# Rotated q and k of the next head pair: the steps of their preparation tied to units of the pair in front

## The chip, the core and the metric

The kernel runs on one core of one Trainium2 chip. A core has five engines with queues of their own that are worked off in order: TensorE (PE in the profile, its weight loads PEld), VectorE (DVE), ScalarE (ACT), GpSimd (POOL) and SyncE (SP), which here issues all DMAs. The metric is the device time of one execution in microseconds; lower is better.

## The reference, cut to what matters

Attention over 4 batches x 8 heads x 576 tokens x 64 channels with a rotary embedding on q and k, then two layers of a two-matrix network on the 2304 tokens:

```
q_rot, k_rot = rotate(q), rotate(k)            # x1*cos - x2*sin, x1*sin + x2*cos
scores = scale * q_rot @ k_rot^T ; scores -= max(scores)
attn = exp(scores) / (sum(exp(scores)) + 1e-9) ; x = attn @ v
h = x @ w_in  (512 -> 2048) ; g = piecewise square of h ; x = g @ w_out
h = x @ w_in2 ; r = max(h, 0) ; out = (s * r*r + b) @ w_out2
```

## The kernel before

**Attention, by pairs and units.** The 32 heads are worked in 16 pairs (one batch, two heads on 64 + 64 partitions). A pair has 9 units of 128 rows of the score matrix (`UNITS`; the fifth unit holds the last 64 rows of both heads). For each unit `qk` lets PE form the scores in one of two PSUM buffers (`sc`), DVE takes the negated maximum (`nm`, L359), ACT the exponential (`p`, L364); two units later PE transposes the result (`tp`), DVE or ACT copies it out (`pt`), and PE multiplies by v (`av`). Scores of a unit can start when the exponential two units earlier has freed its PSUM buffer. Units and pairs are counted from 0 here; "the fourth unit" is k == 3.

**q and k of a pair.** Each is loaded as a tile of 128 x 2 x 576 f32 (the value and its half-swapped copy) into a ring of 4 buffers, `qkin`. `rope_pair` multiplies by the table (POOL, 4 pieces of 288 columns by `pool_tt`, L96), adds the two halves (for q on DVE, L294; for k on POOL, 2 pieces), and splits the result into a rounded part and a low remainder, because PE multiplies in fp32r. For q, `lay_q` does this per head: an ACT copy scaled by 0.125 (L308), then a DVE subtraction (L309), straight into `qs_t[i % 2]`. For k, `lay_k` does one ACT cast (L321), 2 POOL subtractions (the low part), and then 4 DMAs that lay the rounded part into `kh` (L326) and 2 DMAs that lay the low part into `kz` (L329).

**Order of the work.** The main loop runs over units n = 9*i + k and calls in the order "qltaf": scores, loads and preparation (`do_load`), transposes, products with v, and fill. From n = 48 on fill puts matmuls of the first network between the units; between n = 33 and 106 `convert` splits weights (ACT, DVE and POOL). Which instruction stands where in an engine's queue is fixed before the run by a planner with its own clock: it takes the earliest written instruction whose inputs are ready by that clock. `tc.issue_after(x)` only says that an instruction may not stand ahead of x on x's engine. In the kernel before, the preparation of pair i + 1 is written at k == 0 (q) and k == 2 (k) of pair i, from pair 2 on without any tie. The planner therefore hoists it: in the trace the table product of q of pair i + 3 runs during pair i, the sum right behind it, and the parts of q and the DMAs of k for pair i + 2 stand at the turn from pair i to pair i + 1, when the last scores of pair i have freed `qs_t`, `kh` and `kz`. Pair 0 has its own, already tied order.

After attention (some 440 us) three stages of the networks follow, in which PE runs over weights and tokens.

Of the kernel before, what the change touches and what calls it, by code (L numbers as in the profile page):

```python
# [14 lines left out]
ALU = mybir.AluOpType  # L15
# [51 lines left out]
def kernel(ctx, tc, qq, kk, vv, tab, ww1, ww2, s, b, out):  # L67
    nc = tc.nc
# [16 lines left out]
    def pool_tt(out, in0, in1, op, dim=-1):  # L85

        n = out.shape[dim]
        free = 1
        for x in out.shape[1:]:
            free *= x  # L90
        k = min(n, -(-free // PW))
        for i in range(k):
            c = [slice(None)] * len(out.shape)
            c[dim] = slice(n * i // k, n * (i + 1) // k)
            c = tuple(c)
            m = nc.gpsimd.tensor_tensor(out=out[c], in0=in0[c], in1=in1[c], op=op)  # L96
        return m
# [15 lines left out]
    exps, tps, maxs = {}, {}, {}  # L113

    class Slice:
# [6 lines left out]
        def convert(self, raw, pools, hi, lo):  # L122
            if not wide:
                split(hi, lo, raw, nc.scalar, nc.gpsimd)
                return


            top = raw.bitcast(F32).rearrange("p (n t) -> p n t", t=2)[:, :, 1]
            low = raw.bitcast(U16).rearrange("p (n t) -> p n t", t=4)[:, :, 1]
            pool = pools[self.f * 2 + self.made & 1 if len(pools) > 1 else 0]  # L130
            a = pool.tile([P, HW], F32, tag="wa", name="wa", bufs=WB)
            m = pool.tile([P, HW], F32, tag="wm", name="wm", bufs=WB)
            au, mu = a.bitcast(U32), m.bitcast(U32)
            nc.scalar.activation(a, top, AF.Copy, scale=2.0 ** -112)
            nc.vector.tensor_scalar(out=mu, in0=au, scalar1=3, scalar2=None, op0=ALU.logical_shift_left)
            nc.vector.scalar_tensor_tensor(out=mu, in0=au, scalar=0x80000000, in1=mu, op0=ALU.bitwise_and, op1=ALU.bitwise_or)
            nc.vector.tensor_scalar(out=au, in0=mu, scalar1=0xFF800000, scalar2=None, op0=ALU.bitwise_and)
            nc.vector.scalar_tensor_tensor(out=a, in0=low, scalar=2.0 ** -36, in1=a, op0=ALU.mult, op1=ALU.mult)
            nc.scalar.copy(hi, m)  # L139
            pool_tt(out=m, in0=m, in1=hi, op=ALU.subtract)  # L140
            pool_tt(out=lo, in0=m, in1=a, op=ALU.add)
# [106 lines left out]
    tab_sb = att.tile([P, 2, S], F32, name="tab_sb")  # L248
# [4 lines left out]
    qk_in, v_in, stacks = {}, {}, {}  # L253

    WHOLE = [slice(0, S)]
    HALVES = [slice(0, 288), slice(288, S)]

    def load_qk(i, nm, pieces=WHOLE):
        bb, hp = divmod(i, NP)
        t = att2.tile([P, 2, S], F32, tag="qkin", name=f"{nm}in", bufs=QB)  # L260
        for c in pieces:
            nc.sync.dma_start(out=t[:, :, c], in_=(qq if nm == "q" else kk)[bb, hp, :, :, c])
        qk_in[nm, i] = t

    def load_v(i):
        bb, hp = divmod(i, NP)
        t = att2.tile([P, 5, 2, D], F32, tag="vin", name="vin", bufs=VB)
        for out, src in ((t[:, :, 1], vv[bb, hp, :, :, 1]), (t[:D, :4, 0], vv[bb, hp, D:, :4, 0]), (t[D:, :4, 0], vv[bb, hp, :D, 1:, 0]), (t[D:, 4, 0], vv[bb, hp, :D, 0, 0])):
            nc.sync.dma_start(out=out, in_=src)
        v_in[i] = t  # L270
# [15 lines left out]
    def rope_pair(i, nm, mul, add, lo_eng, pieces=WHOLE):  # L286

        t = qk_in[nm, i]
        tt = {nc.gpsimd: pool_tt, nc.vector: nc.vector.tensor_tensor}
        last = None  # L290
        for c in pieces:
            tt[mul](out=t[:, :, c], in0=t[:, :, c], in1=tab_sb[:, :, c], op=ALU.mult)
            r = t[:, 1, c]
            tt[add](out=r, in0=t[:, 0, c], in1=r, op=ALU.add)  # L294
            last = (lay_q if nm == "q" else lay_k)(i, t, c, lo_eng)
        return last

    SELF = [slice(0, D), slice(D, P)]
    laid, parts = set(), {}

    def lay_q(i, t, c, lo_eng, heads=range(2)):

        st = stacks["q", i] = qs_t[i % 2]
        r = t[:, 1, c]
        for j in heads:
            own, other = SELF[j], SELF[1 - j]
            at = slice(j * QW + c.start, j * QW + c.stop)
            h = nc.scalar.activation(st[own, at], r[own], AF.Copy, scale=0.125)  # L308
            m = nc.vector.scalar_tensor_tensor(out=st[other, at], in0=r[own], scalar=0.125, in1=st[own, at], op0=ALU.mult, op1=ALU.subtract)  # L309
        return h.ins, m.ins  # L310

    def lay_k(i, t, c, lo_engs, heads=range(2)):
        if (i, "k") not in laid:
            laid.add((i, "k"))
            stacks["k", i] = att.tile([P, 2, S], F32R, tag="kh", name="kh", bufs=2), kz_t[i % 2]
        kh, kz = stacks["k", i]
        tt = {nc.gpsimd: pool_tt, nc.vector: nc.vector.tensor_tensor}
        r = t[:, 1, c]
        if i > 0:
            hi, lo = t[:, 0, c].bitcast(F32R), r.bitcast(F32R)  # L320
            cast = nc.scalar.copy(hi, r)  # L321
            low = pool_tt(out=lo, in0=r, in1=t[:, 0, c], op=ALU.subtract)
            parts[i] = cast.ins, low.ins
            for j in range(2):
                for rows in SELF:
                    m = nc.sync.dma_start(out=kh[rows, j, c].bitcast(F32), in_=t[SELF[j], 0, c])  # L326
            with tc.issue_after(m.ins):
                for j in range(2):
                    m = nc.sync.dma_start(out=kz[SELF[j], j, c].bitcast(F32), in_=t[SELF[j], 1, c])  # L329
            return m.ins  # L330
        for j in heads:
            own, other = SELF[j], SELF[1 - j]
            nc.scalar.copy(kh[own, j, c], r[own])
            m = nc.scalar.copy(kh[other, j, c], r[own])
            low = tt[lo_engs[j]](out=kz[own, j, c], in0=r[own], in1=kh[own, j, c], op=ALU.subtract)
        return m.ins, low.ins
# [192 lines left out]
    def turned_by(t, c):  # L529
        nc.vector.tensor_tensor(out=t[:, :, c], in0=t[:, :, c], in1=tab_sb[:, :, c], op=ALU.mult)  # L530
        return nc.vector.tensor_tensor(out=t[:, 1, c], in0=t[:, 0, c], in1=t[:, 1, c], op=ALU.add).ins
# [53 lines left out]
    def do_load(n):  # L585
        if n == 0:
            with tc.issue_after(turned):
                turned_by(tq, QP[1])
                lay_q(0, tq, QP[1], None)
        elif n in (1, 2):  # L590
            with tc.issue_after(maxs[n]):
                if n == 1:
                    turned_by(tq, QP[2])
                else:
                    lay_q(0, tq, QP[2], None)
        if n < len(units):
            i, k = units[n]
            if i + 1 < NPAIR:
                if i == 0 and k in (2, 6):
                    with tc.issue_after(maxs[k]):  # L600
                        turned_by(qk_in["q", 1], HALVES[k // 6])
                if i == 0 and k in (4, 5, 7, 8):
                    with tc.issue_after(maxs[k]), tc.issue_after(exps[k - 1]):
                        lay_q(1, qk_in["q", 1], HALVES[k // 6], None, [int(k in (5, 8))])
                if i and k == 0:
                    with ExitStack() if i > 1 else tc.issue_after(parts[1][1]), ExitStack() if i > 1 else tc.issue_after(maxs[9]):
                        rope_pair(i + 1, "q", nc.gpsimd, nc.vector, None)
                elif k == 2:
                    with ExitStack() if i else tc.issue_after(exps[2]), ExitStack() if i else tc.issue_after(lowest):
                        rope_pair(i + 1, "k", nc.gpsimd, nc.gpsimd, [nc.gpsimd, nc.vector])  # L610
                elif k == 7:
                    load_v(i + 1)
                elif k in (4, 6) and i + 2 < NPAIR:
                    load_qk(i + 2, "q" if k == 4 else "k")

        if n in range(33, 51, 2) or n in range(70, 110, 4):
            with tc.issue_after(exps[n - 14]):
                convert()

        if n in PARK_AT and parking:  # L620
            with tc.issue_after(exps[n - 4]):
                parking.pop(0).park(wst, scratch)()
# [31 lines left out]
    def do_fill(n):  # L654
        if n < 48:
            return
        with tc.issue_after(exps[min(n, len(units)) - 4]):
            run_fill(0.62 if n < 76 else 0.92)

    acts = {"q": do_qk, "l": do_load, "t": do_t, "a": do_av, "f": do_fill}  # L660
    for n in range(len(units) + LA):
        with ExitStack() as st:
# [541 lines left out]
```

## Time and profile before

| | |
|---|---|
| median of 3 runs | 1116.61 us (1113.03 to 1118.2) |
| the profiled execution | 1117.65 us, span 1115.9 us, granted TensorE clock 0.998 |
| busy share of the span | PE 96%, PEld 88%, DVE 69%, ACT 57%, POOL 38% |
| pairs 1 to 14, whose code changes | from 33 us to about 440 us |

A row of the trace reads: start in us, length in us, engine, line, operation, out<-in, shapes, count, and in brackets the idle time of the engine before it with what ended it. Rows of waits read: engine, line, what it waited for, then total us, number of times and longest.

### The profile page before, as it was taken

The numbers are of one execution on the slowest core, as the hardware profiler recorded it, in microseconds if no ns is written. First come the engines' busy times: TensorE is split into PE (matmuls) and PEld (weight loads), VectorE is DVE, ScalarE is ACT, GpSimd is POOL, SyncE is SP. The second block draws the span as 40 slices with busy tenths as digits, with TensorE's granted clock in tenths as the row PEclk, the third lists the DMA queues.
The fourth block names the chain that finished last, engine by engine and source line by source line (L and its number), as shares of the span: only waits on it lengthen the run. The fifth ranks groups of instructions, "written<-read, shape, count | busy, mean of one in ns | idle before, by whom it ended". The sixth has DMA issues, their size and how long they took to land.

```text
span 1115.9 us, 20052 instructions
## 1 busy us (share of the span) xinstructions
PE 1074.3 (96%) x7296; PEld 981.3 (88%) x7296; DVE 775.0 (69%) x1445; ACT 631.0 (57%) x1440; POOL 426.9 (38%) x564
## 2 busy tenths in 40 slices
PE   5899999989999999999999999999999999999998
PEld 3666788878888889999999999999999999999997
DVE  7888987768576663454757667866777778677754
ACT  5777776766666665454545455474554448334431
POOL 6998977686473332332544445110212110000000
PEclk9999999999999999999999999999999999999999
DMA  8665856656675544655465673231322853221221
GB/s 240 168 191 167 253 160 208 207 165 188 202 227 166 174 151 138 220 171 190 149 183 203 211 238 116 86 112 59 113 89 90 301 171 116 82 83 42 80 63 36
DMA packets 109762, 173.24 MB, mean 155 GB/s; under 512 B 29408, under 2 KB 80608, under 8 KB 109664
## 3 DMA queue, kind: packets, MB, share of 16 engines
q1 hardware_dynamic: 109664, 171.97, 49.1%
q8 instruction: 57, 0.93, 0.4%
q14 instruction: 41, 0.34, 0.1%
HBM read 110.10 MB, written 48.56 MB: 142 GB/s over the span
## 4 chain that ended last, share of the span: by engine, by line
PE 81%; DVE 5%; DMA 5%; POOL 3%; ACT 3%; issue 2%; SPq 0%; POOLq 0%; ACTq 0%
PE hps L181 15%; PE sum L940 14%; PE yps L856 6%; PE yps L855 6%; PE yps L854 6%; PE y L181 5%; PE sc L357 5%; PE yps L790 4%; PE yps L791 4%; PE yps L792 4%; PE av L405 4%; PE h L181 4%; PE tp L379 3%; DMA wraw<-in_ww 1%; DMA kz<-kin 1%
## 5 line engine op out<-in xcount | busy, mean ns | idle before, releaser
L181 PE MATMUL hps<-xh,w 128*128 128x288 f32 (+4 forms) x640 | 163.4, 324 | 0.0
L357 PE MATMUL sc<-kh,qs 128*128 128x288 f32 x336 | 102.7, 328 | 24.5 <-ACT p L364 13.5
L359 DVE TENSOR_REDUCE nm<-sc 128x1 f32<-128x576 f32 x144 | 106.5, 748 | 24.9 <-PE sc L357 24.4
L364 ACT ACTIVATE p<-sc,nm 128x576 f32<-128x576 f32 x144 | 106.7, 742 | 28.6 <-DVE nm L359 26.2
L948 ACT ACTIVATE four<-four,b_sb,s_sb 128x480 f32<-128x480 f32 x64 | 47.4, 782 | 127.2 <-DVE four L947 127.2
L856 PE MATMUL yps<-gh,w 128*128 128x480 f32 (+1 forms) x320 | 118.5, 370 | 0.0
L854 PE MATMUL yps<-gh,w 128*128 128x480 f32 (+1 forms) x320 | 118.4, 370 | 0.0
L855 PE MATMUL yps<-gl,w 128*128 128x480 f32 (+1 forms) x320 | 118.4, 370 | 0.0
L96 POOL TENSOR_TENSOR wm<-wm,w 128x256 f32<-128x256 f32 x80 | 69.5, 888 | 119.1 <-ACT w L139 62.5
L181 PEld LDWEIGHTS hps<-xh,w 128*128 128x128 f32 x640 | 113.2, 188 | 1.0
L357 PEld LDWEIGHTS sc<-kh,qs 128*128 128x128 f32 x336 | 63.5, 192 | 45.7 <-ACT p L364 27.0
L181 PE MATMUL hps<-xl,w 128*128 128x288 f32 (+4 forms) x320 | 103.7, 324 | 0.0
L790 PE MATMUL yps<-gh,w 128*128 128x288 f32 (+3 forms) x288 | 93.2, 324 | 1.4 <-DVE yp L797 0.7
L357 PE MATMUL sc<-kz,qs 128*128 128x288 f32 x336 | 93.8, 301 | 0.0
L791 PE MATMUL yps<-gl,w 128*128 128x288 f32 (+3 forms) x288 | 92.8, 322 | 0.0
L792 PE MATMUL yps<-gh,w 128*128 128x288 f32 (+3 forms) x288 | 92.8, 322 | 0.0
L379 PE MATMUL tp<-ident,p 128*128 128x128 f32 x576 | 87.2, 276 | 4.0 <-DVE pt L386 3.4
L96 POOL TENSOR_TENSOR wm<-wm,raw 128x256 f32<-128x256 f32 x16 | 12.6, 806 | 176.8 <-ACT raw L139 176.8
L181 PE MATMUL y<-gh,w 128*128 128x288 f32 x320 | 75.0, 305 | 2.0 <-DVE ptr L397 0.9
L379 PEld LDWEIGHTS tp<-ident,p 128*128 128x128 f32 x576 | 70.5, 142 | 6.2 <-DVE pt L386 4.1
L405 PE MATMUL av<-pt,vin 128*64 128x256 f32 (+1 forms) x512 | 75.7, 417 | 0.0
L107 DVE TENSOR_TENSOR gl<-hps,gh 128x288 fp32r<-128x288 f32 (+4 forms) x88 | 46.4, 527 | 40.4 <-ACT gh L103 40.2
(154 smaller groups left out, 2905.9 us busy)
## 6 DMA issues: line engine op xcount, KB each, us to landing
wraw<-in_ww SPq DMA_DIRECT2D x56, 512.0 KB, 4.4
w<-parkd SPq DMA_DIRECT2D x24, 512.0 KB, 6.1
kin<-in_k SPq DMA_DIRECT2D x15, 576.0 KB, 4.4
qin<-in_q SPq DMA_DIRECT2D x15, 576.0 KB, 4.8
kh<-kin SPq DMA_DIRECT2D x60, 144.0 KB, 2.9
parkd<-wraw SPq DMA_DIRECT2D x16, 512.0 KB, 3.2
xs<-y1d SPq DMA_DIRECT2D x32, 240.0 KB, 2.7
xd<-u SPq DMA_DIRECT2D x16, 288.0 KB, 2.7
```

The lines of the kernel that those rows point to most:

```text
L181: m = nc.tensor.matmul(out_ps, l, r, start=(i == 0), stop=(i == n - 1))
L357: nc.tensor.matmul(sc[:, half, o:o + n], l, r[:, k0:k0 + n], start=m == 0, stop=m == len(todo) - 1)
L364: exps[i * 9 + k] = nc.scalar.activation(p, sc[:, :, :288], AF.Exp, bias=nm, scale=1.0, accum_out=sums_t[i][:, col:col + 1]).ins
L379: m = nc.tensor.transpose(v[:, c, :], p[:, c * P:(c + 1) * P], ident)
L405: nc.tensor.matmul(ps[j * D:(j + 1) * D, :n], v[:, kt, j, :], pt[g][:, kt, j, :], start=kt == 0, stop=False)
L790: nc.tensor.matmul(acc, wh, gh, start=f == 0, stop=False)
L791: nc.tensor.matmul(acc, wh, gl, start=False, stop=False)
L792: nc.tensor.matmul(acc, wl, gh, start=False, stop=last)
L854: nc.tensor.matmul(acc, wh, gh, start=f == 0, stop=False)
L855: nc.tensor.matmul(acc, wh, gl, start=False, stop=False)
L856: nc.tensor.matmul(acc, wl, gh, start=False, stop=last)
L940: nc.tensor.matmul(acc, l, r, start=j == 0, stop=j == len(t) - 1)
```

## The change

For pairs i >= 1 the call of `rope_pair` is taken apart. q of pair i + 1: the table product on POOL stays written at k == 0; the DVE sum is written at k == 4 behind the maximum of the unit before (k == 3); the two heads' parts are written at k == 5 and k == 6, their DVE half behind the maximum of the unit before and their ACT half behind the exponential two units before. k of pair i + 1: product and sum on POOL stay at k == 2; cast, low part and the six DMAs are written at k == 3, the cast behind the exponential of k == 2. The tie that q's sum of pair 2 had to the maximum of unit 9 is gone with the call.

```
+                if i:
+                    t = qk_in["q", i + 1]
+                    if k == 0:
+                        with ExitStack() if i > 1 else tc.issue_after(parts[1][1]):
+                            pool_tt(out=t, in0=t, in1=tab_sb, op=ALU.mult)
+                    elif k == 4:
+                        with tc.issue_after(maxs[n - 1]):
+                            nc.vector.tensor_tensor(out=t[:, 1], in0=t[:, 0], in1=t[:, 1], op=ALU.add)
+                    elif k in (5, 6):
+                        with tc.issue_after(maxs[n - 1]), tc.issue_after(exps[n - 2]):
+                            lay_q(i + 1, t, WHOLE[0], None, [k - 5])
                 if i and k == 0:
-                    with ExitStack() if i > 1 else tc.issue_after(parts[1][1]), ExitStack() if i > 1 else tc.issue_after(maxs[9]):
-                        rope_pair(i + 1, "q", nc.gpsimd, nc.vector, None)
+                    pass
                 elif k == 2:
                     with ExitStack() if i else tc.issue_after(exps[2]), ExitStack() if i else tc.issue_after(lowest):
-                        rope_pair(i + 1, "k", nc.gpsimd, nc.gpsimd, [nc.gpsimd, nc.vector])
+                        if i == 0:
+                            rope_pair(i + 1, "k", nc.gpsimd, nc.gpsimd, [nc.gpsimd, nc.vector])
+                        else:
+                            t = qk_in["k", i + 1]
+                            pool_tt(out=t, in0=t, in1=tab_sb, op=ALU.mult)
+                            pool_tt(out=t[:, 1], in0=t[:, 0], in1=t[:, 1], op=ALU.add)
+                elif k == 3 and i:
+                    with tc.issue_after(exps[n - 1]):
+                        lay_k(i + 1, qk_in["k", i + 1], WHOLE[0], None)
```

## Rows read from the trace of the kernel before

**Rows 1.** Busy us by engine in two stretches: PE, PEld, DVE, ACT, POOL; clock, DMA.
```profile
33.00:440.00 407.00, 384.89 (x2920) 323.05 (x2919) 298.33 (x529) 282.96 (x693) 260.88 (x352) 1.00 0.61 184
440.00:1116.00 676.00, 670.25 (x4279) 643.76 (x4277) 451.73 (x880) 328.01 (x701) 142.41 (x172) 1.00 0.41 135
```
**Rows 2.** The same view, pair 2 alone (first maximum to first maximum).
```profile
53.53:71.89 18.36, 18.05 (x132) 12.85 (x132) 15.97 (x28) 13.73 (x34) 16.50 (x21) 1.00 0.67 188
```
**Rows 3.** Waits of PE between 33 and 440 us, the longest group.
```profile
PE sc L357 <- ACT p L364: 10.4, 13, 1.9
```
**Rows 4.** Instructions on tile qin (ns min/median/max), then who waited for it.
```profile
L308 ACT ACTIVATE qs<-qin x38: 306/681/695, 8.3 to 361.6; 64x576 fp32r<-64x576 f32 x28, 64x288 fp32r<-64x288 f32 x4, 64x192 fp32r<-64x192 f32 x2, 64x128 fp32r<-64x128 f32 x2
L309 DVE SCALAR_TENSOR_TENSOR qs<-qin,qs x38: 284/754/1354, 8.7 to 363.8; 64x576 fp32r<-64x576 f32 x28, 64x288 fp32r<-64x288 f32 x4, 64x192 fp32r<-64x192 f32 x2, 64x128 fp32r<-64x128 f32 x2
...
L294 DVE TENSOR_TENSOR qin<-qin x14: 879/1266/1345, 33.9 to 315.6; 128x576 f32<-128x576 f32 x14
...
  DVE qin L294: 12.3, 7
...
  DVE qs L309: 5.5, 8
  ACT qs L308: 3.1, 4
```
**Rows 5.** Timeline of pair 1: q's sums, an exponential, and PE's gaps.
```profile
33.86 1.33 DVE L294 TENSOR_TENSOR qin<-qin 128x576 f32<-128x576 f32 x1
...
36.57 0.66 PE L379 MATMUL tp<-ident,p 128*128 128x128 f32 x4 [1.03 <-DVE pt L386]
...
38.59 1.24 DVE L294 TENSOR_TENSOR qin<-qin 128x576 f32<-128x576 f32 x1
...
40.54 0.74 ACT L364 ACTIVATE p<-sc,nm 128x576 f32<-128x576 f32 x1 [1.82 <-DVE nm L359]
...
41.42 0.40 PE L357 MATMUL sc<-kh,qs 128*128 128x288 f32 x1 [1.69 <-ACT p L364]
```
**Rows 6.** Timeline of pair 4: q's sum, one of q's parts, and PE's gaps.
```profile
101.51 1.27 DVE L294 TENSOR_TENSOR qin<-qin 128x576 f32<-128x576 f32 x1 [1.88 <-POOL qin L96]
...
104.09 0.44 PE L392 MATMUL tr<-ident,p 128*128 128x128 f32 x2 [0.70 <-DVE pt L386]
...
108.27 0.68 ACT L308 ACTIVATE qs<-qin 64x576 fp32r<-64x576 f32 x1
...
109.86 0.40 PE L357 MATMUL sc<-kh,qs 128*128 128x288 f32 x1 [1.19 <-ACT p L364]
```
**Rows 7.** Timeline of pairs 7 to 9: three gaps of PE, and the longest wait of a sum.
```profile
181.76 0.40 PE L357 MATMUL sc<-kh,qs 128*128 128x288 f32 x1 [1.91 <-ACT p L364]
...
195.78 0.66 PE L379 MATMUL tp<-ident,p 128*128 128x128 f32 x4 [0.69 <-DVE pt L386]
...
226.76 1.27 DVE L294 TENSOR_TENSOR qin<-qin 128x576 f32<-128x576 f32 x1 [3.45 <-POOL qin L96]
...
230.65 0.40 PE L181 MATMUL h<-xh,w 128*128 128x288 f32 x1 [1.33 <-ACT pt L384]
```
**Rows 8.** Timeline: first scores of pairs 2 and 4, third exponential of pair 3.
```profile
51.59 0.40 PE L357 MATMUL sc<-kh,qs 128*128 128x288 f32 x1 [0.27 <-ACT p L364]
...
78.00 0.74 ACT L364 ACTIVATE p<-sc,nm 128x576 f32<-128x576 f32 x1 [0.43 <-DVE nm L359]
...
89.04 0.40 PE L357 MATMUL sc<-kh,qs 128*128 128x288 f32 x1
```
**Rows 9.** Timeline and tile kin: issue of kz, a cast, its low part, landing times.
```profile
55.80 1.10 SPq L329 DMA_DIRECT2D kz<-kin  x2
...
111.86 0.67 ACT L321 CAST kin<-kin 128x576 fp32r<-128x576 f32 x1
...
116.03 1.73 POOL L96 TENSOR_TENSOR kin<-kin 128x288 fp32r<-128x288 f32 x2
...
DMA to landing us min/median/max: 2.3/3.8/7.0
```

## Prediction, made before the change was run

> **What bounds the kernel now.** I read first the busy times by stretch [rows 1]. From 440 us on PE is busy 670.25 of 676 us at full clock: whatever comes earlier out of attention is kept to the end, because nothing behind it but PE decides. Between 33 and 440 us, where the changed pairs run, PE is busy 384.89 of 407 us. It stands idle for 22.1 us in all, so even a perfect change gains no more than that by this row. An undisturbed pair shows the same: pair 2 takes 18.36 us, of which PE works 18.05 [rows 2]. The change removes no work from any engine; it can only turn PE's gaps into work, or make new ones.
>
> Next come PE's waits there. The largest group is scores that wait for an exponential, 10.4 us at 13 places [rows 3]. Then the tile of q [rows 4]: the DVE sum sat waiting 12.3 us at 7 places for the table product on POOL, the DVE half of the parts 5.5 us for its ACT half, the ACT half 3.1 us for what stood before it. These are waits on DVE and ACT, whose queues run in order, so a maximum or a copy behind the waiting instruction is late as well. Only what of that reaches PE counts, and that the timeline tells.
>
> **What is removed.** I went through the gaps of PE over 0.25 us between 33 and 440 us (23 of them, 20 us) and kept those with q's sum or parts just ahead on the engine that PE then waits for. In pair 1 two sums (33.86 and 38.59, q of pairs 2 and 3) and their parts stand within 6 us on DVE; PE waits 1.03 us for a copy and 1.69 us for an exponential whose maximum was late [rows 5]. In pair 4 the sum waits 1.88 us and runs 1.27, PE then misses a copy for 0.70 us; later an ACT half of the parts, 0.68 us, stands right ahead of an exponential and PE misses 1.19 us [rows 6]. In pairs 7 to 9 the same patterns give 1.91, 0.69 and 1.33 us, the last after a sum that had waited 3.45 us [rows 7]. Together 1.03 + 1.69 + 0.70 + 1.19 + 1.91 + 0.69 + 1.33 = 8.5 us. That is what can be blamed on this work. The other gaps have weights or the network's own chain ahead of them.
>
> **What stays.** The instructions themselves are not removed: per pair one sum (0.88 us at best, 1.27 at the median) and two heads' parts (0.68 us on ACT and 0.75 on DVE each [rows 4]). Now they stand between the maxima and exponentials of units 4 to 6. There they are spread over three units, and their inputs are long ready: the table product is written at unit 0 and takes 4 short POOL pieces, so the waits of 12.3 us should go. But each still delays a maximum by about 1 us or an exponential by 0.7. Four of the seven gaps come from waiting or from two pairs' work bunched together (1.69, 0.70, 1.33 and part of 1.03), the rest mostly from the plain length of an instruction in front of an exponential (1.19, 1.91, 0.69). So about half goes: between 0 and -8.5 us I take -4.3.
>
> **What is moved: k.** Before, cast, low part and DMAs of k ran a pair or more ahead of use. Now the cast waits in ACT's queue for the third exponential of the pair just in front, and behind it come POOL's low part and SP's six DMAs. Queued behind the cast on ACT are the exponentials of the next units, behind the low part on POOL the weight pieces (POOL is busy 260.88 of 407 us [rows 1]) and behind the DMAs on SP the loads of the next q and k. The chain from that exponential: cast 0.67; wait of the low part on POOL, 0 to 3.5 (a cast that ended at 112.53 had its low part started at 116.03); low part 1.73; issue of two kz DMAs 1.10; landing 3.8 at the median, 2.3 to 7.0 [rows 9]. With 0.8 for POOL's wait, about one piece of other work, that is 0.67 + 0.8 + 1.73 + 1.1 + 3.8 = 8.1 us; the ends are 5.8 and 14.0. It must be over when PE wants the first scores of the next pair. In pair 1 the third exponential ended at 41.28 [rows 5] and the scores of pair 2 started at 51.59: 10.3 us; in pair 3 it was 89.04 - 78.74 = 10.3 [rows 8], and pair 2 is alike. Later pairs last 20 to 33 us, with fill between the units, and have 13 us and more. So the median chain is hidden with 2.2 us to spare in the three short pairs, and the term is 0, with at most 3 x 3.7 = 11 us if everything is late. q's parts have less to do: the second head's copy stands behind the exponential of unit 4, needs 0.68 + 0.75 us, no DMA, and three more units pass before it is used; I cost it at nothing.
>
> **Moved on SP and POOL.** At the turn of a pair SP used to stand with k's DMAs waiting for the last scores to free kh and kz. That wait goes, since the pair before the last has long freed them when the fourth unit comes. The q buffer is freed later, at unit 6 instead of a pair earlier, so the load two pairs on starts later; POOL then gets it about when the next pair begins, still a pair ahead of its sum. I cost both at 0. The changed order shifts everything the planner places; by the nearest rows, gaps of 0.69 to 1.91 us, some three more or fewer of them are +-4 us.
>
> **Sum.** 1117.65 - 4.3 + 0 = 1113.35 us for the profiled execution, which lies 1.04 us above the median of the runs; for the median 1112.3 us.
>
> **The rivals.** *B, the work keeps its price.* PE's gaps at units 4 to 6 replace those at the turns, because a 1.27 us sum or a 0.68 us copy stands in front of a maximum or an exponential wherever it is put. Pair 2, at 18.05 of 18.36 us, has little to give in any case. Then 1116.6, +-2. *C, k comes late.* From the point at which the chain takes more than the 10.3 us of a short pair, PE waits at the head of pairs 2 to 4 for kz, and the units behind it drain. Halfway between the margin's end and the worst case the lateness is about 2 us in each, 6 us in all, and with no gain elsewhere the time is 1122.6; with the worst chain 1127.6. For it: the low part queues on a POOL that is busy 16.50 of 18.36 us in pair 2 [rows 2], and the 3.5 us wait has happened. Against it: in the sum of medians 2.2 us are left over. *D, the room is larger than PE's row shows.* All waits around q count, not only those that I could follow to PE: 12.3 + 5.5 + 3.1 = 20.9 us [rows 4]; half of that would be 10.5 us and 1106.1, all of it 1095.7. Beside this stands the Trainium skill, "Perfetto Trace Analysis", Engine Utilization and the note at its head: matmul busy time is a poor measure because matmuls are pipelined, weight-load busy time a good one. By it attention is far from full: PEld is busy 323.05 of 407 us, 79%, against 95% after 440 us [rows 1], which leaves some 64 us of room, not 22. I side with the PE row, since the row of pair 2 has PE without gaps at a PEld share of only 12.85 of 18.36 us, so weight loads there are short, not late [rows 2].
>
> **How the numbers follow.** A measurement of this kernel tells about 0.5% from no change, 5.6 us: faster is under 1111.0, slower over 1122.2. My forecast (1109 to 1116) has 0.45, of which 0.15 lie under 1111.0; B has 0.17, all within; C has 0.25, of which 0.15 lie over 1122.2; D has 0.13, all under. So faster 0.28, same 0.30 + 0.17 + 0.10 = 0.57, slower 0.15. The range: downward all 8.5 us gone and the planner's 4 us on the good side, 1116.6 - 12.5 = 1104; upward no gain and C with a little more than its 6 us, 1124. Outside lie half of D and a third of C, 0.15.
>
> **What would show it.** Right: the waits of the DVE sum for POOL are gone (12.3 to under 2 us), scores waiting for exponentials fall from 10.4 to about 6 us, PE's idle time between 33 us and the end of attention falls from 22 to about 18 us, and the first scores of a pair wait for no DMA. B: the sum's waits are gone and PE's idle time is still 21 us or more. C: PE's first scores of pairs 2 to 4 wait for kz or kh, 1 to 4 us each. D: PE's idle time is under 12 us. The forecast is wrong altogether if the late stretch after attention changes by more than 2 us, for nothing there depends on this by my reading.

## The result, and the profile of the changed kernel

| | kernel before | changed kernel |
|---|---|---|
| median | 1115.83 us (1111.22 to 1118.5, 20 runs) | 1120.59 us (1116.71 to 1128.81, 20 runs) |
| ratio, with its 95% interval | | 1.0051 [1.0039, 1.0063] |
| profiled execution | 1117.65 us, span 1115.9 us, clock 0.998 | 1119.19 us, span 1117.4 us, clock 0.997 |

The forecast was 1112.3 us, some 4 us less; the measurement is 4.8 us more. By the prediction's own bounds (1111.0 and 1122.2 us) that is about the same time; it lies in the stated range, and the sign is wrong.

The changed kernel by stretch, as in [rows 1] and [rows 2] (columns as there), with pairs 1 and 2 by themselves:

```profile
33.00:440.00 407.00, 385.67 (x2909) 322.35 (x2909) 293.13 (x527) 280.10 (x687) 257.68 (x350) 0.99 0.61 183
440.00:1116.00 676.00, 672.33 (x4295) 645.90 (x4293) 452.76 (x882) 330.48 (x707) 144.47 (x174) 1.00 0.41 136
...
33.97:49.78 15.81, 15.81 (x117) 11.39 (x117) 13.32 (x23) 12.90 (x32) 10.07 (x14) 1.00 0.50 130
49.78:70.27 20.49, 18.73 (x135) 13.01 (x134) 16.91 (x27) 15.12 (x35) 15.64 (x20) 1.00 0.55 167
```

Pair 1 of the kernel before, for comparison:

```profile
33.08:53.53 20.45, 17.36 (x126) 11.81 (x123) 17.80 (x28) 14.96 (x36) 18.68 (x24) 1.00 0.62 177
```

Pair 1 did what the forecast wanted: 20.45 became 15.81 us, with no gap on PE. But POOL worked only 10.07 of 15.81 us in it, against 18.68 of 20.45, and pair 2 already takes 20.49 us where it took 18.36 [rows 2]. Over all of attention PE's idle time is 407 - 385.67 = 21.3 us, against 22.1 before.

PE's waits between 33 and 440 us in the changed kernel (engine, line, what for: total us, times, longest), the row that answers [rows 3]:

```profile
PE sc L357 <- ACT p L364: 6.6, 12, 1.0
```

Tile of q in the changed kernel, as in [rows 4]; q's sum is now line 612, and the rows below it say who waited for the tile:

```profile
L612 DVE TENSOR_TENSOR qin<-qin x14: 748/932/1381, 39.0 to 381.7; 128x576 f32<-128x576 f32 x14
...
  POOL qin L96: 27.1, 6
...
  ACT qs L308: 3.9, 6
  DVE qs L309: 2.0, 2
```

The sum's waits of 12.3 us [rows 4] are gone altogether: no row names line 612. What has come in their place is the first of the rows on waits: POOL's own waits for the tile, by the same view 22.5 us at 9 places before, are 27.1 us at 6, and where they fall matters more. POOL's waits between 33 and 110 us, first of before, then of the changed kernel:

```profile
POOL qin L96 <- DMA qin<-in_q: 3.9, 2, 2.0
POOL kin L96 <- ACT kin L321: 3.5, 2, 2.7
POOL qin L96 <- DVE nm L359: 1.0, 1, 1.0
```

```profile
POOL qin L96 <- DMA qin<-in_q: 12.3, 3, 5.3
POOL vin L275 <- DMA vin<-in_v: 2.4, 1, 2.4
POOL kin L96 <- DMA kin<-in_k: 2.3, 1, 2.3
```

and POOL's busy time (fifth number behind the stretch's length) there, before and changed:

```profile
33.00:110.00 77.00, 70.58 (x510) 49.55 (x509) 65.58 (x107) 58.28 (x138) 67.37 (x88) 1.00 0.62 178
```

```profile
33.00:110.00 77.00, 72.86 (x520) 51.04 (x520) 66.24 (x107) 58.12 (x137) 59.79 (x78) 1.00 0.56 164
```

POOL does 7.6 us less in the first pairs, because it stands waiting for q loads, 12.3 us instead of 3.9. The queue of SP says why. Timeline of SP in pair 1 before, from 38 us on, and of the table product on POOL that waits for the q load:

```profile
38.59 0.33 SPq L262 DMA_DIRECT2D qin<-in_q  x1
38.97 1.10 SPq L329 DMA_DIRECT2D kz<-kin  x2
...
44.12 3.08 POOL L96 TENSOR_TENSOR qin<-qin,tab_sb 128x288 f32<-128x288 f32 x4 [1.03 <-DVE nm L359]
```

and of the changed kernel, with the last of q's parts on DVE that frees the buffer, and the same product:

```profile
38.81 2.66 SPq L326 DMA_DIRECT2D kh<-kin  x4
...
43.81 1.29 DVE L309 SCALAR_TENSOR_TENSOR qs<-qin,qs 64x576 fp32r<-64x576 f32 x1
...
44.51 1.10 SPq L329 DMA_DIRECT2D kz<-kin  x2
45.71 1.96 SPq L269 DMA_DIRECT2D vin<-in_v  x3
...
48.95 1.01 SPq L262 DMA_DIRECT2D qin<-in_q  x1
...
53.70 3.25 POOL L96 TENSOR_TENSOR qin<-qin,tab_sb 128x288 f32<-128x288 f32 x4 [4.93 <-DMA qin<-in_q]
```

The q load issued in pair 1 (the q of pair 4) goes into the buffer of the q whose parts are formed in pair 1. Before, that was over at 38.6 us; now these parts stand at units 5 and 6 of the pair and end at 45.10 us. Behind that, k's second DMAs, which waited for POOL's low part (until 45.61), and the v loads are still ahead of it on SP. It is issued 10.4 us later (48.95 - 38.59): some 6.5 us of that is the later buffer, the rest is SP's queue. POOL starts its next q at 53.70, not at 44.12 us.

### The profile page after: what moved, and what is told of

Same layout as the page of the kernel before. It is cut to its first block, busy times and chain, and to the rows that moved or that the text cites. A ratio compares the mean times of both kernels' runs of the same rounds, so it can differ in the third digit from the quotient of the medians.

```text
span 1117.4 us, 20030 instructions
## 1 busy us (share of the span) xinstructions
PE 1077.1 (96%) x7296; PEld 982.7 (88%) x7296; DVE 770.6 (69%) x1445; ACT 630.1 (56%) x1440; POOL 426.0 (38%) x564
## 4 chain that ended last, share of the span: by engine, by line
PE 81%; DVE 7%; POOL 5%; ACT 4%; issue 2%; DMA 2%; SPq 0%; POOLq 0%; DVEq 0%; ACTq 0%
PE hps L181 15%; PE sum L958 13%; PE yps L874 6%; PE yps L873 6%; PE yps L872 6%; PE sc L357 5%; PE yps L808 4%; PE yps L809 4%; PE yps L810 4%; PE y L181 4%; PE h L181 4%; PE av L405 4%; PE tp L379 3%; DVE nm L359 2%; POOL kin L96 2%
## 5 line engine op out<-in xcount | busy, mean ns | idle before, releaser
L181 PE MATMUL hps<-xh,w 128*128 128x288 f32 (+4 forms) x640 | 163.4, 324 | 0.0
```

Source lines behind the costliest of these rows:

```text
L181: m = nc.tensor.matmul(out_ps, l, r, start=(i == 0), stop=(i == n - 1))
```

## The experiments

The letters in the expectations are the prediction's B, C and D and: W, the first network's weight pieces (split on POOL, DVE and ACT) stand at fixed dates that shortened pairs run into; L, each order of the queues has its own fortune; P, POOL runs dry in the first pairs because loads come later, and lacks that lead when the weight pieces are due. Three letters stand in the earlier expectations: K, k comes too late (the prediction's C); H, TensorE's half-rate stretches make the difference; and P there, up to late6, means something else, namely that the planner's new order makes gaps of its own. Results at a glance; "POOL" is its busy time between 33 and 110 us of the profiled execution, from the view shown above, "8th piece" the time at which POOL ends the eighth weight piece in that execution (164.9 us in the first trace of the kernel before, 167.5 in that of the changed kernel), and "clock" the mean granted clock over all executions of the kernel:

| run | median us | before, same chip | ratio | POOL | 8th piece | clock |
|---|---|---|---|---|---|---|
| before2 | 1113.13 | 1114.99 | 0.999 [0.9976, 1.0003] | 68.87 | 161.7 | 0.997 |
| after2 | 1117.90 | 1113.96 | 1.0038 [1.0019, 1.0057] | 59.83 | 167.5 | 0.996 |
| q_only | 1119.09 | 1113.96 | 1.004 [1.0024, 1.0056] | 66.06 | 163.4 | 0.993 |
| k_only | 1118.85 | 1113.96 | 1.004 [1.0019, 1.006] | 56.55 | 173.7 | 0.994 |
| low_first | 1124.02 | 1113.96 | 1.0084 [1.0069, 1.0098] | 57.60 | 182.0 | 0.993 |
| k_early | 1117.22 | 1114.99 | 1.0023 [1.0008, 1.0039] | 60.31 | 159.2 | 0.994 |
| first6 | 1140.94 | 1114.99 | 1.0235 [1.0218, 1.0253] | 57.72 | 197.4 | 0.985 |
| late6 | 1110.22 | 1114.99 | 0.9963 [0.9945, 0.9982] | 68.13 | 161.5 | 0.998 |
| early5 | 1126.97 | 1115.19 | 1.0112 [1.0094, 1.013] | 60.34 | 181.1 | 0.993 |
| late6_q | 1111.73 | 1115.19 | 0.998 [0.9965, 0.9995] | 66.77 | 165.3 | 0.997 |
| after_w | 1114.16 | 1115.19 | 0.9988 [0.9974, 1.0001] | 65.48 | 150.9 | 0.997 |
| before_w | 1119.20 | 1115.19 | 1.0042 [1.0026, 1.0058] | 68.75 | 163.9 | 0.995 |
| after_w3 | 1118.30 | 1113.50 | 1.0039 [1.0023, 1.0054] | 62.87 | 167.7 | 0.997 |
| after_wl | 1119.56 | 1113.50 | 1.0051 [1.0031, 1.0071] | 57.14 | 175.8 | 0.996 |
| low_first_w | 1123.47 | 1113.50 | 1.0095 [1.0079, 1.0112] | 56.16 | 180.8 | 0.993 |
| late6b | 1107.66 | 1113.50 | 0.9954 [0.9937, 0.9971] | 66.85 | 163.7 | 0.998 |
| before_late | 1129.73 | 1113.43 | 1.0142 [1.0123, 1.016] | 48.54 | 181.5 | 0.988 |
| after_qe | 1108.85 | 1113.43 | 0.9962 [0.9947, 0.9977] | 63.36 | 156.3 | 0.999 |

**The two halves.** `after2` is the changed kernel again; `q_only` has the new q and the old k, `k_only` the old q and the new k:

```
q_only:                elif k == 2: rope_pair(i + 1, "k", ...)     # as before; no lay_k at k == 3
k_only:                if i and k == 0: rope_pair(i + 1, "q", ...) # as before; no q steps at k == 4, 5, 6
```

> The changed kernel once more, unedited, for a second trace of it. Theory K (k's low part waits on POOL and comes too late): again 7 to 10 us from the end of k's cast to the start of its low part in pairs 2 to 5, and the median 4 to 6 us over the kernel before. Theory P (the planner's new order makes POOL late with the network's partial sums in pairs 12 and 13): again two or more gaps of PE over 1 us between 310 and 345 us. Theory H (the clock): the half-rate stretch near 150 us, 6.8 us long in the first trace of this kernel against 3.4 before, differs from execution to execution; if it alone made the difference, a trace with 3.4 us has a span 1.7 us shorter.

> q's sum and parts tied to units as in the changed kernel, k prepared as before the change. Theory K: the loss came with k, so this is as fast as before or faster by 2 to 5 us (1111 to 1116). Theory P: it is slower than before as well, by 2 to 6 us, or anything within 5 us either way, since each new order makes its own gaps. The waits of the DVE sum for POOL are gone by both.

> k's cast and low part moved to the fourth unit as in the changed kernel, q prepared as before. Theory K: slower than before by the 4 to 6 us of the whole change or more (1120 to 1123), and PE's first scores of pairs 4 to 6 stand at the landing of kz. Theory P: as likely faster as slower, within 5 us of before.

Each half alone costs as much as both, so it is not one half that is bad. In k_only POOL waited 17.7 us for k loads between 33 and 110 us; q_only has 3.9 us of such waits, and its loss looks different: its clock is 0.993, against 0.997 before (the last section). The second trace of the changed kernel repeats the first: POOL waits 12.5 us for q loads, k's low part waits 4.1 to 8.1 us in pairs 1 to 5. Of the gaps over 1 us that the planner's theory wanted between 310 and 345 us there were three in the first trace and one in the second.

**Is k late (C)?** In the changed kernel k does come late. Timeline of pair 3 and the head of pair 4: cast, low part, kz issue, first scores:

```profile
76.64 0.67 ACT L321 CAST kin<-kin 128x576 fp32r<-128x576 f32 x1
...
85.46 3.71 POOL L96 TENSOR_TENSOR kin<-kin 128x288 fp32r<-128x288 f32 x4
...
87.05 2.23 SPq L329 DMA_DIRECT2D kz<-kin  x2
...
90.33 0.30 PE L357 MATMUL sc<-kz,qs 128*128 128x288 f32 x1
```

Cast over at 77.31, low part at 85.46: POOL had products and sums of the pair after next ahead in its queue. In pairs 1 to 5 this wait was 4.1, 5.8, 8.2, 6.1 and 6.8 us, and in pairs 3 to 5 the last kz landed 1 to 2 us behind the first scores. `low_first` ties those products behind the low part; `k_early` forms k two units sooner. `before2`, the kernel before again, ran beside them:

```
low_first:  with tc.issue_after(parts[i][1]): pool_tt(...)    # q's product; k's product and sum
k_early:    -elif k == 2:             +if k == (0 if i else 2):        # product and sum
            -elif k == 3 and i:       +elif k == 1 and i:              # cast, low part, DMAs
```

> The changed kernel with one thing more: on POOL the products of q and k of pair i + 1 may not stand ahead of the low part of k of pair i, so that the low part no longer queues behind some 8 us of the next pair's products. Theory K: from the end of the cast to the start of the low part under 2 us, kz lands 5 us earlier, and most of the loss of 4.8 us comes back (1115 to 1117). Theory P: the low part is early, and the time stays at 1119 to 1122 or moves by another order's gaps.

> The kernel before once more, unedited, for a trace of it on this chip. Theory H (TensorE's half-rate stretches, which follow clusters of PE's gaps, carry most of the difference between the kernels): one half-rate stretch of 3.4 us near 150 us, as in its first trace, and a mean granted clock of 0.997 to 0.998 over its executions, against 0.993 to 0.996 for the others. Theory K has no opinion. Time as before, within 1 us.

> The changed kernel with k asked for two units sooner: product and sum at unit 0, cast and low part at unit 1 behind the exponential of unit 0. Theory K: kz lands 4 us or more ahead of the first scores of pairs 3 to 6, where it was 1 to 2 us late; 2 to 4 us come back (1115 to 1117). Theory H: the time follows the half-rate stretches of the new order; with a mean clock of 0.995 or less it stays at 1118 or more although kz is early.

before2, at 0.999, shows how far no change can stray. In low_first and k_early kz landed 3 to 10 us ahead of the first scores (low_first 4 to 7), and both stay slower than before; low_first is even slower than the changed kernel, k_early gets at most a part of the loss back. C's condition is met in the changed kernel, but taking it away does not bring the time of before back. Where low_first lost is plain; PE's waits between 110 and 200 us, and POOL's longest between 33 and 110 us:

```profile
PE y L181 <- POOL w L96: 5.1, 2, 4.9
PE sc L357 <- ACT p L364: 4.6, 6, 1.4
```

```profile
POOL kin L96 <- ACT kin L321: 10.4, 4, 2.6
```

A weight piece of the first network that POOL had not yet split held PE for 4.9 us. So POOL's lateness, not k's, came into view. Here it has a cause of its own: the new ties let POOL wait 10.4 us for k's cast, and it waits for no load.

**Which pairs?** `early5` has the new order in pairs 1 to 5 only, `first6` the same with low_first's ties, `late6` from pair 6 on only, and `late6_q` q alone from pair 6 on:

```
early5, first6:  -if i:   +new = 0 < i < 6 ; if new: ...   (else the calls of before)
late6, late6_q:  -if i:   +new = i >= 6 ; if new: ...
```

> The changed order, with the low part kept ahead of the next pair's products on POOL, for pairs 1 to 5 only; from pair 6 on all as before the change. Theory K: the short pairs gain 3 us as in the trace of the kernel with that tie throughout (its transposes were 3.0 us ahead of the kernel before at 110 us), and nothing is lost later: 1110 to 1112, faster than before by 2 to 4 us. Theory H: the gain at 110 us is the same, and what arrives at the end is decided by half-rate stretches between 140 and 260 us: anything from 1110 to 1119, with base (time less half the half-rate time) 2 to 3 us under the kernel before.

> The changed order from pair 6 on only; pairs 1 to 5 as before the change. Theory K: pairs from 6 on have 15 us and more for the chain and kz is never late, so this is as fast as before within 2 us (1112 to 1116). Theory H and P: it is slower by 2 to 5 us, from gaps and half-rate stretches between 150 and 345 us, with no first scores that wait for kz.

> The other half of the split: the changed order for pairs 1 to 5, all as before from pair 6 on. Theory W (with the early pairs reordered, the weight pieces of the first network, which POOL, DVE and ACT split during pairs 3 to 7, come later and PE's fill in pairs 6 and 7 waits for them): slower than before by 4 to 10 us, the transposes 3 to 10 us behind at 190 us and no further behind after that; eighth weight piece on POOL at 167 us or later, against 162 to 165 before. Theory K would have the same sign, with the loss in pairs 3 to 6 before 135 us. If the loss of the whole change were in its late pairs, this would be as fast as before.

> Of the version that is changed from pair 6 on only: q's part alone, k as before. The first prediction's step (the sum no longer waits for the product on POOL) lies in q, so by it the gain of 4 us stays: 1110 to 1112. If the gain came with k's DMAs leaving the turn of the pair, or from the planner's new order as such, 1113 to 1117.

The late pairs gain, which none of the theories had expected: late6 is faster than both kernels, and q alone gives half of it or more (3.5 of 4.8 us). The early pairs lose more than that: against before2, early5 had PE 0.4 us behind at the 30% mark of the transposes (109 us) and 15.6 us behind at the halfway mark (207 us; 11.4 us against the first trace of the kernel before). Its PE waits between 110 and 200 us again name the pieces, and so does, below them, the same view of first6, which is 26 us slower than before and the slowest of all:

```profile
PE sc L357 <- ACT p L364: 5.8, 6, 3.2
PE y L181 <- POOL w L96: 3.2, 1, 3.2
```

```profile
PE y L181 <- POOL w L96: 12.7, 2, 6.9
```

**The dates of the weight pieces (W).** `after_w`, `after_w3` and `after_wl` write the first nine pieces 6 and 3 units sooner and 6 later; `before_w` and `low_first_w` take the 6 sooner into before and low_first:

```
-if n in range(33, 51, 2) or n in range(70, 110, 4):
+if n in range(27, 45, 2) or n in range(70, 110, 4):   # _w; _w3: range(30, 48, 2); _wl: range(39, 57, 2)
```

> The changed kernel with the first nine splits of weights asked for six units sooner (units 27 to 43 instead of 33 to 49). Theory W: the eighth piece is ready by 155 us, PE's fill in pairs 6 and 7 waits less, and 2 us or more of the loss come back: 1113 to 1116. Theory H: the time goes by the half-rate stretches, 1114 to 1121.

> The kernel before with the same nine splits six units sooner, as the control of the run above. Theory W: the pieces are in time here anyway or nearly so (eighth piece 2 to 3 us ahead of its use), so it gains at most 2 us: 1112 to 1115. If sooner pieces help both kernels alike, theory W does not explain the difference between them.

> The changed kernel with its first nine weight pieces written three units earlier (units 30 to 46 instead of 33 to 49). If the weight pieces are what the shorter pairs run into (theory W), a half of the way of the six units gives a half or more of the 4 us back: 1114 to 1116 where the changed kernel has some 1118.5 and the kernel before some 1115. If the gain of six units was the fortune of one order of the queues (rival L), this one can land anywhere from 1114 to 1123, with no relation to the date.

> The changed kernel with the same pieces written six units later (units 39 to 55). W: TensorE's fill waits more for them, 3 to 8 us slower than the changed kernel, 1121 to 1126, with new gaps of the network's matmuls behind POOL's weight pieces. L: anywhere from 1114 to 1123.

> The run with POOL's low part of k ahead of its next table products (1124 us), with the weight pieces six units earlier. There TensorE waited 4.86 and 1.69 us for weight pieces in pair 7, and the eighth piece was done at 182.0 us. W: these waits go and 5 to 8 us come back, 1116 to 1119, the more so as this order has k in time by 4 to 7 us; L: no more than 2 us come back.

after_w was 4 to 6 us faster than the changed kernel and before_w lost 4 us, which looked like W. The doses say no: three sooner gave nothing, six later cost at most 2 us instead of 3 to 8, and low_first_w got 0.6 of the 5 to 8 us back. The reason is in the trace. Writing a piece sooner does not by itself make POOL do it sooner: the eighth piece was done at 167.5 us in the changed kernel, at 167.7 in after_w3 and at 180.8 in low_first_w (182.0 in low_first), but at 150.9 in after_w. Of these only after_w also has POOL at work for 65.48 us in the first pairs. W as first put falls; what stays of it is that POOL is behind.

**POOL's lead (P).** `before_late` changes nothing in what is written of the kernel before but the place of the q and k loads in SP's queue in pairs 1 to 5; `after_qe` moves q's three steps of the changed kernel three units forward, which frees q's buffer sooner; `late6b` is late6 again:

```
before_late: -elif k in (4, 6) and i + 2 < NPAIR:  load_qk(i + 2, ...)          # for i in 1..5
             +elif k == 8: with tc.issue_after(v_last[0]): load_qk(i + 2, "q"); load_qk(i + 2, "k")
after_qe:    -elif k == 4: (sum)    -elif k in (5, 6): (parts)
             +elif k == 1: (sum)    +elif k in (2, 3): (parts)
```

> The kernel before, with nothing changed but the loads of the next q and k: in pairs 1 to 5 they stand on SP behind the v loads, where the changed kernel has them; q's sum and parts and k's preparation stay where they were. Theory P (POOL runs dry in pairs 1 to 3 because loads come later, and misses that lead when the first network's weight pieces are due): POOL is busy about 60 of the 77 us from 33 to 110 us, as in the changed kernel (59.8), not 67 to 69 as before, its waits for q and k are over 8 us, and the time is 3 to 6 us more than before, 1117 to 1120. Rival L (each order has its own fortune, or the steps' new places cost by themselves): 1112 to 1116, as before.

> The changed kernel with q's sum at the second unit and its parts at the third and fourth, three units sooner, which frees q's buffer sooner; k as in the changed kernel. P: the q loads stand ahead of k's DMAs on SP, POOL's waits for q fall from 12.3 us to under 6, POOL is busy 63 us or more from 33 to 110 us, and 1 to 4 us of the changed kernel's loss come back: 1113 to 1117 where before has 1114. L: no relation, 1116 to 1122.

> The changed order from pair 6 on alone, pairs 1 to 5 as before, once more: if the gain is one of the kernel and not of one chip's hour, the ratio is again 0.995 to 0.998, 1110 to 1113 us where the kernel before has 1115.

before_late, busy times and clock, the loads of q of pairs 3 and 4 on SP, POOL's two longest waits between 33 and 110 us, then PE's waits between 33 and 440 us:

```profile
33.00:110.00 77.00, 68.44 (x454) 47.99 (x453) 60.73 (x95) 52.39 (x122) 48.54 (x65) 0.91 0.47 138
```

```profile
47.16 0.58 SPq L262 DMA_DIRECT2D qin<-in_q  x1
...
72.96 0.58 SPq L262 DMA_DIRECT2D qin<-in_q  x1
```

```profile
POOL vin L277 <- PE av L414: 7.8, 1, 7.8
POOL qin L96 <- DMA kin<-in_k: 5.3, 1, 5.3
```

```profile
PE sc L359 <- ACT p L366: 12.1, 14, 2.3
PE sc L359 <- DMA kz<-kin: 7.0, 2, 4.2
```

after_qe, busy times, then POOL's waits to 110 us, then PE's to 440 us:

```profile
33.00:110.00 77.00, 71.61 (x515) 50.17 (x514) 66.74 (x109) 58.48 (x139) 63.36 (x83) 1.00 0.62 171
33.00:440.00 407.00, 389.26 (x2959) 327.90 (x2958) 305.42 (x535) 284.93 (x705) 269.51 (x355) 1.00 0.63 188
```

```profile
POOL qin L96 <- DMA qin<-in_q: 2.0, 2, 1.4
```

```profile
PE sc L357 <- ACT p L364: 7.0, 7, 1.3
```

Later loads alone, with every step of q and k written where it was, make the kernel before 16 us slower, three to five times what P expected, where L expected nothing. But the dose is not that of the changed kernel. There q of pair 4 is loaded at 48.95 us, here at 72.96 (38.59 before); over pairs 3 to 7 the q loads are 19 to 46 us later than before, in the changed kernel 0 to 17 us. And it works in other ways too: k's own preparation is late (7.0 us of PE waiting for kz), POOL's longest wait is one for PE, its waits for q and k loads are 6.1 us where P expected over 8, and TensorE loses clock, 0.91 in this stretch. So before_late shows that late loads cost time in this kernel, and not what those of the changed kernel cost.

after_qe is nearer to the question. Its q loads are 0 to 6 us later than before, POOL waits 2.0 instead of 12.3 us for q, and it is 4.6 us faster than the kernel before and some 9 to 10 us faster than the changed kernel (ratios 0.9962 against 1.0038 and 1.0051). P expected 1 to 4 us of that. As the sum and the parts have moved as well as the loads, the gain is that of the whole move. late6b confirms late6.

What stays open. A run that would separate the two, after_qe with its q loads held back to where the changed kernel has them, was not made. P by busy time orders the table only roughly: q_only and before_w lose 4 us or more with POOL at 66 and 69 us; k_early, the changed kernel and early5 all have it at 60 and cost 2, 4 to 5 and 12 us; after_qe is faster than before with 63. The date of the eighth piece orders it better. All nine runs in the table that have it after 166 us are slower than before, by 0.4 to 2.4%; of the nine that have it earlier six are as fast or faster, and the exceptions are q_only, k_early and before_w, in the first two of which most of the loss goes with the clock (the last section). That late pieces then hold PE is seen in early5, low_first and first6. In the changed kernel itself no row shows PE waiting for a weight piece: between 110 and 200 us its waits are at most 2.8 us for one cause (scores for exponentials). Its PE does not stand idle longer either: 21.3 and 20.8 us between 33 and 440 us in its two traces, 22.1 and 19.2 in those of the kernel before. The place of the loss can be named: from 33 to 110 us the changed kernel does no fewer matmuls (520 and 520, against 510 and 520), but it does fewer in the next 60 us. That stretch in before, before2, the changed kernel and after2:

```profile
110.00:170.00 60.00, 55.93 (x416) 46.90 (x417) 51.01 (x90) 45.09 (x109) 50.03 (x65) 0.97 0.71 213
110.00:170.00 60.00, 56.74 (x437) 46.96 (x435) 52.43 (x90) 44.06 (x107) 53.25 (x69) 1.00 0.74 230
110.00:170.00 60.00, 55.70 (x401) 45.90 (x400) 46.56 (x84) 44.07 (x106) 53.20 (x71) 0.94 0.70 206
110.00:170.00 60.00, 53.63 (x394) 44.15 (x390) 47.79 (x84) 42.40 (x104) 52.31 (x69) 0.97 0.70 207
```

The changed kernel does 15 to 43 matmuls fewer there, at a lower clock in part of it, and from 33 to 440 us it does 8 to 37 fewer, so nearly all of the loss is there by 170 us. That POOL's lost 7.6 us are the reason is the account that fits most runs; it is argued and not traced piece by piece. A deeper ring of q and k buffers, which would take the dependence away, was not tried.

## Why the prediction was wrong, point by point

**What bounds the kernel.** Right in its first half: nothing after attention changed by itself. From the last transposes to the end it is 689.4 and 688.7 us in the two traces of the kernel before, 688.8 and 688.1 in those of the changed kernel; the stages there start later by what attention lost. Incomplete in its second: from PE's row I took POOL for an engine with room. Its 260.88 of 407 us [rows 1] are an average; in pairs 1 to 4 (33 to 110 us) it is busy 67.37 of 77 us, and so nearly as full as PE (70.58). The 16.50 of 18.36 us of pair 2 were in front of me [rows 2], and I used them only against the low part of k.

**What is removed, -4.3 us.** Right in sign, and near in size where the loads stay early. The sum's waits are gone, scores waiting for exponentials fell from 10.4 to 6.6 us (forecast about 6), and the two versions that keep the loads early gain 4.6 us (after_qe: 1113.43 - 1108.85) and 4.8 to 5.8 us (late6 and late6b). In after_qe PE's idle time is 407 - 389.26 = 17.7 us, the "about 18" of the forecast. That the sizes agree is in part luck: late6 leaves pairs 1 to 5 as they were, where 4.61 of the 8.5 us of gaps stand; half of the remaining 3.93 would be 2 us, and q alone gained 3.5 (late6_q), q and k 4.8 and 5.8. In the changed kernel PE's idle time is 21.3 us, the sign that was given for B.

**What is moved: k, 0 us.** The term that was mis-sized is POOL's wait ahead of the low part: 0.8 us taken, 3.5 the end, 4.1 to 8.2 measured, because products and sums of the pair after next are ahead of it in POOL's queue. I had counted "one piece of other work". The chain took 9.4 to 15.9 us in pairs 1 to 5, against 8.1 forecast and 10.3 of margin; pairs 3 to 5 were late, by about 2 us at most, and PE filled most of that with other matmuls. C came true in its condition, and low_first and k_early show that it is not the whole cause: with kz in time both are still slower than before.

**Moved on SP and POOL, 0 us.** This is the step that failed, as far as the runs tell. "The q buffer is freed later ... so the load two pairs on starts later; POOL then gets it about when the next pair begins, still a pair ahead of its sum. I cost both at 0." The chain was right, and nearly its date (53.70 us, with the next pair's first maximum at 49.78); the price was not. I asked whether the sum would get its product in time (it did) and not what POOL would do instead while the load was not there. It stood waiting for q loads for 12.3 us, where it had had 9.6 us of idle time in all, and did 7.6 us less in the first pairs. With q's steps three units sooner these waits are 2.0 us, and the kernel is 9 to 10 us faster. By which way POOL's lost time reaches the end of the changed kernel stays open; that its lead over the weight pieces was the cover, which the text did not name, is the account that fits most runs. I had also named the loads that stand behind k's DMAs on SP, and given them no price: k's DMAs now wait there for the cast and the low part, and the q load comes behind them and the v loads (38.81 to 48.95 us).

**The planner's +-4 us.** It was entered as chance. In early5, low_first and first6 a part of the loss is not chance: PE waits 3.2, 5.1 and 12.7 us for weight pieces that POOL had not done. What no theory here explains is of the size given (before_w, 4 us).

**The rivals.** B's sign showed in the profile, but not its reason: the work in its new place can gain. D set 20.9 us of waits around q against PE's row; the best versions reach -4.6 to -5.8 us, a fifth to a good quarter of that. The Trainium skill, "Perfetto Trace Analysis", Identifying the Most-Contended Engine, judges TensorE's headroom by its share of peak FLOPs and by the busy share of weight loads; from the latter the prediction's estimate was some 64 us. No run here came near it, and after_qe, with PE idle for 17.7 us, has weight loads for 327.90 of 407 us, 81%. Two rivals were missing: an engine off the path that loses its lead, the one that the runs point to, and the clock, which had no term in the sum and goes with 0.9 us (after2) of the loss.

**The chances.** Slower had 0.15, all of it from C at its worst. With a price for POOL's idle time, from its 67.37 of 77 us in the first pairs, I would have given a loss as much as the gain.

## What to carry to other kernels

When a step moves later, ask which buffer it holds, which load waits for that buffer, which engine reads that load, and what that engine does meanwhile. Here it was POOL, busy 67.37 of 77 us in the first pairs, and no row of PE's waits showed it as a bound. Average busy time over a long stretch hides this: read the share of each engine in the first pairs, where the lead is built. And try such a move at several places and in parts: three units sooner turned +0.4% into -0.4%, and the late pairs alone gained 0.4 to 0.5%. When a control is built, read its dates in the trace: before_late held the loads back much further than the change did.

## What the runs showed of the hardware

TensorE's clock moves the time of some versions by as much as the change did. Changed kernel, granted clock (the number behind the five engines) in slices of 2 us:

```profile
150.00:152.00 2.00, 1.59 (x9) 1.06 (x7) 1.97 (x5) 2.00 (x7) 2.00 (x4) 0.79 1.05 167
152.00:154.00 2.00, 1.15 (x5) 1.15 (x6) 2.00 (x5) 2.00 (x6) 2.00 (x3) 0.50 0.93 313
154.00:156.00 2.00, 2.00 (x10) 1.99 (x10) 1.65 (x4) 1.63 (x6) 0.80 (x2) 0.50 1.01 408
156.00:158.00 2.00, 2.00 (x10) 1.98 (x10) 1.25 (x2) 1.40 (x4) 2.00 (x4) 0.50 0.52 184
```

and PE's gaps around its fall (in brackets, with what ended them):

```profile
149.47 0.66 PE L379 MATMUL tp<-ident,p 128*128 128x128 f32 x4 [1.24 <-ACT pt L384]
150.53 0.40 PE L357 MATMUL sc<-kh,qs 128*128 128x288 f32 x1 [0.41 <-ACT p L364]
152.85 0.61 PE L181 MATMUL y<-gh,w 128*128 128x288 f32 x1 [0.86 <-ACT pt L382]
```

The clock goes from its full 2.4 to 1.2 GHz (0.50) here for 6.8 us. The 0.79 of the first slice puts the fall at about 151.2 us; the gaps of 1.24 and 0.41 us lie ahead of it, that of 0.86 us behind it. Such stretches last 3.4 to 20.5 us in these traces, in the kernel before as well, and one kernel differs from one execution to the next (0.991 to 1.000 in after2). Within one kernel, over 261 executions, the time grows by 0.74 us for each us by which the mean clock falls short of full (one minus the clock, times the span). The Trainium skill, "TensorE: Matmul & The Clock Gate", Terms, puts the penalty at the throttled time times the share of clock missing in it, by which the estimate would be 1 us here. The runs show somewhat less.

At 0.74 the clock goes with 3.4 of the 4.9 us by which the mean of q_only lies over that of before, 2.5 of 2.9 in k_early, 7.9 of 16.0 in before_late, and 0.9 of 4.5 in after2: most of the loss in the first two, half in the third, a fifth in the changed kernel. So the half-rate stretches alone (H) do not explain the change. Why q_only's gaps fall so that the clock drops is open.
